# Transposes of 66 rows in place of 40 in the one-layer steps of a recurrent-memory transformer kernel

## The chip, the cores and the metric

The kernel runs on one core of one Trainium2 chip. The metric is the device time of one execution in microseconds (us); of several runs the median is taken. Besides these runs there is one profiled execution, which has its own time. In its trace every instruction has an engine, a line of the kernel, a start and a duration. The engines are PE (TensorE, matmuls), PEld (its weight loads), DVE (VectorE), ACT (ScalarE), POOL (GpSimd) and SP (SyncE, which here only issues DMAs).

## The reference: what is computed

Two layers of a transformer with a recurrent memory, each followed by a gated feed-forward network. The sequence of 2048 rows of width 512 is cut into 64 segments of 32 rows. Each segment is put behind 8 memory rows, so one segment has 40 rows (L = 40 in the code), and 32 heads of width 128 attend within these 40 rows. The first 8 rows of the attention's output are the memory of the next segment: that is the recurrence.

```python
for s in range(n_seg):                      # 64 segments
    xs = x[:, s * seg_len:(s + 1) * seg_len, :].copy()
    h = jnp.concatenate([mem, xs], axis=1)  # 8 + 32 rows
    q = jnp.einsum('btd,dhe->bhte', h, Wq)  # k and v likewise
    scores = jnp.einsum('bhqe,bhke->bhqk', q, k) * scale
    scores = jnp.where(mask[None, None], scores, -1000000000.0)
    p = _softmax(scores, axis=-1)
    o = jnp.einsum('bhqk,bhke->bhqe', p, v)
    o = jnp.einsum('bhte,hed->btd', o, Wo)
    mem = o[:, :M, :].copy()
    outs.append(o[:, M:, :])
...
x = x + A(_layernorm(x)); x = x + B(_layernorm(x))     # layer 0
x = x + A(_layernorm(x)); x = x + B(_layernorm(x))     # layer 1, same weights
```

B is `(sigmoid(x @ w_gate) * (x @ w_up)) @ w_down` with 1792 hidden columns. Data is bf16.

## The kernel before

**Steps.** The two layers run interleaved: step t (`emit_step`, L771) works on segment t of layer 0 and on segment t - 6 of layer 1 (LAG = 6), so there are 70 steps. Steps 6 to 63 are two-layer steps: the 40 rows of both layers stand side by side, 80 columns (`ncol` = 80, `both` true). Steps 0 to 5 have layer 0 alone and steps 64 to 69 layer 1 alone: these 12 are the one-layer steps, with `ncol` = 40. After every fourth step the feed-forward network of a block of 128 rows (`ffn`, L1050) is added for each layer, and projections of values (`v_pass`, `strips`, `v_half`) for later steps are spread among all of it.

**Inside a step.** The 32 heads are cut into groups. In one-layer steps there are two rows of 16 heads; a group takes three heads of each row (five groups of six heads), and the last group takes one of each (two heads). For each group:

- q and k for three heads at a time on PE (L868), copied to SBUF by ACT (L891, recorded at L1228), then the scores on PE (L904).
- Softmax: the mask is added on DVE (L918), the maximum taken (L923) and subtracted (L925), the exponential on ACT (L928), its sum (L930), its reciprocal (L932), and the weights written by DVE to the tile `pb` (L939, `pmul`). `pb` is 80 partitions by 3 by 128: a partition is a query row, and in one-layer steps each of the (up to) three blocks of 128 columns holds the 40 keys of two heads side by side, the rest zero.
- Transposes on PE (L950, `ptr`): for each block one transpose, whose stationary operand is the block and whose moving operand is a corner of the identity. `full` (L783) says how many partitions are read; it has the size `ncol`, so 40 in one-layer steps and 80 in two-layer steps. The result has 128 partitions and as many columns as rows were read, and block ul starts at column ul x 80 (LW = 80) of a PSUM bank.
- The copies out of PSUM to `ptsb` (L954, `spread`) on ACT or DVE, which read the first 40 columns of each 80; then weights times values on PE (L976), a copy on ACT (L985), and the output projection on PE (L995), which sums all heads of the step in one bank.

At the end of a step DVE copies the new memory rows into the input of the next step (L1013, in two-layer steps L1008), and ACT copies the others (L1020). The first q and k of the next step wait for it.

So a one-layer step has 5 x 3 + 1 = 16 transposes, and the 12 of them have 192. The 58 two-layer steps have 11 each, 638 in all, of 80 rows.

**Order.** All work is recorded as tasks with `pl.add(engine, duration, function, reads, writes)`. The order over all engines isn't searched for in the kernel: it is decoded from a packed list, `SEQUENCE` (L53, decoded in `plan`, L249), and with it for some copies the choice between ACT and DVE. The durations given to `pl.add` are used by `replay` (L268) only to reckon start times; from these come the pace at which POOL issues the large weight loads (a load waits for a PE task) and a few fill-in matmuls in reckoned gaps of PE (`warm`, L332). `mm_ns(n)` is the reckoned duration of a matmul with n columns. Each engine runs its own instructions in the order given and waits on semaphores for the others.

**Contents of `pb`.** Its three buffers are set to zero at the start (`clear`, L496). One-layer steps write partitions 0 to 39, two-layer steps 0 to 79.

## Time and profile before

| what | us |
|---|---|
| median of 3 runs | 1756.25 |
| lowest and highest of them | 1754.74, 1759.64 |
| profiled execution, its own time | 1757.29 |
| its span in the trace | 1755.3 |

Stretches of the same trace, by the view of windows:

| stretch, us from the start | what runs | length | PE busy |
|---|---|---|---|
| 60 to 172 | steps 0 to 5, with the end of the loading of weights at the front | 112.00 | 110.64 |
| 172 to 1624 | two-layer steps | 1452.00 | 1448.62 |
| 1624 to 1740 | steps 64 to 69 | 116.00 | 115.05 |

How to read it: the span is the time from the first to the last instruction in the trace; the time of an execution is a little more. Busy time of PE is the union of its matmuls, whose ends are modelled; matmuls overlap in the pipeline, so a single duration (some 180 to 200 ns for a small one) is far more than the distance from one start to the next, and it is this distance that PE pays for a matmul. In a form such as `40*128 40x40 bf16` the first number is the rows of the stationary operand (the contraction), the second its columns, and `40x40` is the moving operand, partitions by columns. A timeline row merges equal instructions that follow each other: its start, its duration to the end of the last, and how many. The granted clock is 1.00 (full) in all three stretches.

### The profile page before, as it was taken

The page shows a single profiled execution, that of the slowest core. Times are in us where ns is not written, and L with a number is a line of the kernel's source. Part 1 is how long each engine was busy: PE and PEld are TensorE (multiplying, and loading weights), DVE is VectorE, ACT ScalarE, POOL GpSimd, SP SyncE. Part 2 cuts the span into 40 slices and gives each one's busy share as a digit, 9 for nine tenths or more (in the row PEclk, how much of TensorE's full clock was granted, in tenths as well). Part 3 has the DMA queues.
Part 4 walks back from the last instruction along what each step waited for, and adds up shares of the span by engine and source line. Part 5 has one row for each costly group of instructions (what it writes and reads, how often), then busy time and mean ns, then how long its engine had stood idle before and what let it go on. Part 6 is the DMA issues. An engine that isn't in the chain of part 4 may idle for free.

```text
span 1755.3 us, 91842 instructions
## 1 busy us (share of the span) xinstructions
PE 1743.5 (99%) x39162; PEld 1496.5 (85%) x39162; DVE 1249.4 (71%) x4208; ACT 1129.5 (64%) x3119; POOL 856.8 (49%) x1367
## 2 busy tenths in 40 slices
PE   9999999999999999999999999999999999999999
PEld 4688889889898988989888888989888898989887
DVE  5667777677777776786677767776777777767676
ACT  3576777566666766666666656666665666666554
POOL 6524345635544554445455563554455463554443
PEclk9999999999999999999999999999999999999999
DMA  9935455635645555545455564545455464554644
GB/s 299 307 95 150 110 153 154 200 110 152 176 130 163 156 160 142 166 127 166 146 148 159 141 178 125 167 138 152 135 166 170 133 179 126 147 156 128 170 116 136
DMA packets 145583, 273.41 MB, mean 156 GB/s; under 512 B 39686, under 2 KB 86018, under 8 KB 145174
## 3 DMA queue, kind: packets, MB, share of 16 engines
q0 software_dynamic: 72944, 198.79, 39.6%
q1 hardware_dynamic: 72230, 68.75, 13.3%
q8 instruction: 307, 5.03, 1.2%
q14 instruction: 102, 0.84, 0.2%
HBM read 221.78 MB, written 27.07 MB: 142 GB/s over the span
## 4 chain that ended last, share of the span: by engine, by line
PE 96%; DMA 2%; DVE 1%; POOL 0%; SPq 0%; issue 0%; ACT 0%; POOLq 0%; ACTq 0%
PE bank L868 34%; PE bank L995 17%; PE bank L1097 11%; PE bank L762 8%; PE bank L635 7%; PE bank L1120 6%; PE bank L904 4%; PE bank L976 4%; PE bank L950 2%; PE bank L595 1%; PE bank L1214 1%; DMA wk_sb<-in_A_Wk_dram 1%; PE bank L1065 0%; DMA scr<-wu 0%; DMA wq_sb<-in_A_Wq_dram 0%
## 5 line engine op out<-in xcount | busy, mean ns | idle before, releaser
L868 PE MATMUL bank<-hT,wq_sb 128*128 128x80 bf16 (+3 forms) x8960 | 616.4, 198 | 2.4 <-DMA wq_sb<-in_A_Wq_dram 1.6
L868 PE MATMUL bank<-hT,wk_sb 128*128 128x80 bf16 (+3 forms) x8960 | 616.1, 198 | 1.0 <-DMA wk_sb<-in_A_Wk_dram 1.0
L1228 ACT CAST qku<-bank 128x480 bf16<-128x480 f32 (+4 forms) x770 | 384.6, 508 | 225.2 <-PE bank L868 196.2
L868 PEld LDWEIGHTS <-wq_sb 128*128 128x128 bf16 x8960 | 454.1, 99 | 33.7 <-issue 14.8
L868 PEld LDWEIGHTS <-wk_sb 128*128 128x128 bf16 x8960 | 446.8, 99 | 1.1 <-DMA wk_sb<-in_A_Wk_dram 1.1
L918 DVE TENSOR_TENSOR st<-bank,cst 40x240 f32<-40x240 f32 (+3 forms) x768 | 280.3, 368 | 116.5 <-PE bank L904 103.3
L995 PE MATMUL bank<-otsb,wo_sb 128*128 128x80 bf16 (+1 forms) x8960 | 360.4, 198 | 0.0
L995 PEld LDWEIGHTS <-wo_sb 128*128 128x128 bf16 x8960 | 335.9, 99 | 13.3 <-issue 0.2
L1228 ACT CAST otsb<-bank 128x480 bf16<-128x480 f32 (+3 forms) x420 | 200.4, 483 | 90.5 <-PE bank L976 60.3
L1090 POOL DMA_DIRECT2D wu<-in_B_w_up_dram x217 | 166.1, 766 | 172.2 <-PE bank L950 39.0
L1114 POOL DMA_DIRECT2D wd<-in_B_w_down_dram x217 | 156.5, 721 | 185.3 <-PE bank L1120 40.1
L1224 POOL DMA_DIRECT2D vsb<-sst x351 | 177.8, 511 | 130.5 <-ACT sst L1228 62.9
L1089 POOL DMA_DIRECT2D wg<-in_B_w_gate_dram x217 | 166.0, 765 | 140.6 <-PE bank L1097 58.8
L928 ACT ACTIVATE st<-st 80x240 f32<-80x240 f32 (+3 forms) x420 | 159.1, 381 | 56.5 <-DVE st L925 53.7
L1097 PE MATMUL bank<-xnT,wg 128*128 128x128 bf16 (+2 forms) x1784 | 171.6, 218 | 0.0
L1097 PE MATMUL bank<-xnT,wu 128*128 128x128 bf16 (+2 forms) x1784 | 171.0, 218 | 0.0
L930 DVE TENSOR_REDUCE small<-st 80x6 f32<-80x240 f32 (+3 forms) x420 | 151.3, 362 | 25.8 <-ACT st L928 22.3
L1220 ACT ACTIVATE ptsb<-bank,small 120x160 bf16<-120x160 bf16 (+3 forms) x430 | 156.7, 386 | 19.2 <-PE bank L950 12.5
L904 PE MATMUL bank<-qku 128*128 128x80 bf16 (+1 forms) x2240 | 162.8, 197 | 0.5 <-issue 0.4
L925 DVE TENSOR_TENSOR st<-st,small 80x240 f32<-80x240 f32 (+3 forms) x420 | 154.8, 370 | 5.7
L939 DVE TENSOR_TENSOR pb<-st,small 80x240 bf16<-80x240 f32 (+3 forms) x420 | 153.9, 369 | 5.7
L923 DVE TENSOR_REDUCE small<-st 80x6 f32<-80x240 f32 (+3 forms) x420 | 152.4, 363 | 6.2
(108 smaller groups left out, 2551.6 us busy)
## 6 DMA issues: line engine op xcount, KB each, us to landing
wg<-in_B_w_gate_dram POOLq DMA_DIRECT2D x220, 256.0 KB, 4.1
wu<-in_B_w_up_dram POOLq DMA_DIRECT2D x220, 256.0 KB, 4.2
wd<-in_B_w_down_dram POOLq DMA_DIRECT2D x220, 256.0 KB, 3.9
vsb<-scr SPq DMA_DIRECT2D x137, 66.0 KB
scr<-vst SPq DMA_DIRECT2D x90, 96.0 KB
vsb<-scr POOLq DMA_DIRECT2D x93, 66.0 KB, 3.5
vsb<-sst SPq DMA_DIRECT2D x179, 32.0 KB
vsb<-sst POOLq DMA_DIRECT2D x169, 32.0 KB, 2.8
```

The lines of the kernel that those rows point to most:

```text
L868: nc.tensor.matmul(o_ap, lhsT=W[:, c, h * P:(h + 1) * P], rhs=mv(c), start=(c == 0), stop=(c == DC - 1))
L904: nc.tensor.matmul(s_all(SB)[:, w0 + i, :], lhsT=fview(qku[:, i, 0, 0:1], [(1, P)]), rhs=qku[:, i, 1, 0:ncol], start=True, stop=True)
L918: pl.add("DVE", dve_ns(n, True), lambda gsz=gsz, hs=hs, st=st, SB=SB, pj_=pj_, npj_=npj_, mk=mk, idx=idx: nc.vector.tensor_tensor(out=st[p ...
L928: pl.add("ACT", act_ns(n), lambda hs=hs, st=st: nc.scalar.activation(out=st[pr, hs], in_=st[pr, hs], func=ACTF.Exp, scale=self.scale), r=s ...
L995: nc.tensor.matmul(WB[:, c * ncol:(c + 1) * ncol], lhsT=self.wo[:, h, c * P:(c + 1) * P], rhs=otsb[:, hl, 0:ncol], start=(h == 0 and c == ...
L1089: pl.add("POOL", 760, lambda wg=wg, fs=fs: nc.gpsimd.dma_start(out=wg[:], in_=self.wgv[:, :, fs]), r=[("wo", self.H - 1)], w=[gk] + bt, la ...
L1090: pl.add("POOL", 760, lambda wu=wu, fs=fs: nc.gpsimd.dma_start(out=wu[:], in_=self.wuv[:, :, fs]), r=[("wo", self.H - 1)], w=[uk] + bt, la ...
L1097: nc.tensor.matmul(gu[:, 2 * i + k, 0:n], lhsT=W[:, c, i * P:(i + 1) * P], rhs=xnT[:, c, rw], start=(c == 0), stop=(c == DC - 1))
L1114: pl.add("POOL", 760, lambda wd=wd, ip=ip: nc.gpsimd.dma_start(out=wd[:], in_=self.wdv[:, 2 * ip:2 * ip + 2, :]), w=[dk] + (["boot"] if se ...
L1220: nc.scalar.activation(out=dst, in_=src, func=ACTF.Copy, scale=by)
L1224: {"SP": nc.sync, "POOL": nc.gpsimd}[tk.on].dma_start(out=got[1], in_=got[2])
L1228: nc.scalar.copy(out=dst, in_=src)
```

## The change

The slice `full` becomes 66 in one-layer steps in place of 40; it stays 80 in two-layer steps. With it the transposes of one-layer steps read 66 partitions of `pb`, use a corner of the identity of 66 x 66, and write 66 columns of each block of 80 in PSUM. The duration given for the task is that of 66 columns.

```diff
-        full = slice(0, ncol)
+        full = slice(0, LW if both else 66)
...
                 for ul in range(nu):
-                    nc.tensor.transpose(out=pt[:, ul * LW:ul * LW + ncol], in_=pb[full, ul, :], identity=self.ident[full, full])
-
-            pl.add("PE", nu * mm_ns(ncol), ptr, r=[("pb", bi)], w=[PB])
+                    nc.tensor.transpose(out=pt[:, ul * LW:ul * LW + full.stop], in_=pb[full, ul, :], identity=self.ident[full, full])
+
+            pl.add("PE", nu * mm_ns(full.stop), ptr, r=[("pb", bi)], w=[PB])
```

The rows 40 to 65 that are now read hold zeros in steps 0 to 5, and in steps 64 to 69 what the last two-layer step that used the buffer left there. They meet the columns 40 to 65 of the identity, so they go to columns 40 to 65 of the result, which the copies to `ptsb` don't read. Every engine's list of instructions, and what each of them waits for, is the same in both programs; the 192 transposes (a load of weights and a matmul each) differ in size alone.

## The prediction

> **What bounds the kernel now.** I read the page first: busy time by engine, then the chain that ended last.

> ```profile
> PE 1743.5 (99%) x39162; PEld 1496.5 (85%) x39162; DVE 1249.4 (71%) x4208; ACT 1129.5 (64%) x3119; POOL 856.8 (49%) x1367
> ...
> PE 96%; DMA 2%; DVE 1%; POOL 0%; SPq 0%; issue 0%; ACT 0%; POOLq 0%; ACTq 0%
> ```

> TensorE (PE) issues nearly all the time, and 96% of the chain of waits is PE. But a busy PE can still be a slow one: a matmul counts as busy until its modelled end, so a hole of 0.1 us between two starts stays invisible here. The second reading is therefore where the changed transposes stand, by the view of line L950 in the two stretches of one-layer steps (60 to 180 us, and 1624 to 1740 us), and the busy time of those stretches.

> ```profile
> L950 PE MATMUL bank<-cst,pb x96: 176/176/190, 62.1 to 167.6; 40*128 40x40 bf16 x96
> ```

> ```profile
> L950 PE MATMUL bank<-cst,pb x96: 176/176/190, 1633.0 to 1736.8; 40*128 40x40 bf16 x96
> ```

> ```profile
> 60.00:172.00 112.00, 110.64 (x2908) 89.23 (x2909) 78.53 (x277) 77.30 (x279) 43.24 (x72) 1.00 0.55 162
> 172.00:1624.00 1452.00, 1448.62 (x32279) 1272.90 (x32268) 1047.50 (x3529) 956.47 (x2546) 716.96 (x1120) 1.00 0.53 150
> 1624.00:1740.00 116.00, 115.05 (x3273) 98.11 (x3272) 83.25 (x290) 69.28 (x230) 54.84 (x82) 1.00 0.53 149
> ```

> The columns are the stretch, its length, then busy us of PE, PEld, DVE, ACT, POOL, the granted clock, DMA share, GB/s. So 192 transposes of 40 rows exist, all in stretches where PE is busy for 110.64 of 112 us and 115.05 of 116 us at a clock of 1.00, while DVE and ACT are at 60 to 72%. What a PE instruction costs there is what the kernel pays.

> Third, the timeline of PE, starts in us, then duration. First 80-row transposes between other matmuls (a two-layer step), then 40-row ones (a one-layer step).

> ```profile
> 1612.64 0.31 PE L868 MATMUL bank<-hT,wq_sb 128*128 128x80 bf16 x4
> 1612.78 0.31 PE L868 MATMUL bank<-hT,wk_sb 128*128 128x80 bf16 x4
> 1612.93 0.24 PE L950 MATMUL bank<-cst,pb 80*128 80x80 bf16 x2
> 1613.01 0.31 PE L868 MATMUL bank<-hT,wq_sb 128*128 128x80 bf16 x4
> ```

> ```profile
> 1632.50 0.39 PE L1097 MATMUL bank<-xnT,wg 128*128 128x128 bf16 x4
> 1632.72 0.39 PE L1097 MATMUL bank<-xnT,wu 128*128 128x128 bf16 x4
> 1633.04 0.24 PE L950 MATMUL bank<-cst,pb 40*128 40x40 bf16 x3
> 1633.21 0.27 PE L868 MATMUL bank<-hT,wq_sb 128*128 128x40 bf16 x4
> ```

> Four 128-column matmuls take 0.22 us from start to start (1632.50 to 1632.72). Before the 40-row transposes the same four take 0.32 (1632.72 to 1633.04): 0.10 us of hole. Then three transposes hold PE for 0.17 us, though they are half as wide as the 80-row ones, two of which take 0.08. Around the 80-row ones nothing is lost: 0.14 to 0.15 us for the four in front, as for the four before. [...]

> **The change, part by part.** I call a run of L950 transposes with other matmuls on both sides a visit. The trace has 67 visits with 192 transposes of 40 rows: 10 of one transpose, 52 of three, 2 of four, 3 of six. All distances are from start to start.

> *Removed: the entry hole.* What stands before a visit normally moves on after 25 ns (L995, L904 and L868 at 40 or 54 columns), 35 (L976 at 80), 56 (L1097 at 128) or 216 (512 columns). Before a visit it takes 112, 111, 117, 130, 152 and 310. The excess is 87 to 96 ns, and 6.13 us over the 67.
> *Replaced: the transposes.* Inside a visit the 125 distances sum to 3.91 us (31 ns each); from a visit's last transpose to the next matmul it is 109 ns (122 in a visit of one), 7.58 us in all. Before: 6.13 + 3.91 + 7.58 = 17.62 us of PE.
> *Added: 26 columns and 26 rows.* No 66-row transpose is in the trace. Lower bound: a plain matmul with 66 columns (L868 128x66) moves on after 29 ns. Upper bound without a hole: an 80-row transpose with 80 columns takes 40. 66 columns lie a little nearer the first, so 33 inside a visit, and 29 for the last one, since the last of an 80-row visit goes at its plain matmul pace (35). After: 125 x 33 + 67 x 29 = 4.13 + 1.94 = 6.07 us; with 29 and 40 inside it is 5.57 and 6.94.
> *Does 66 behave as 80 or as 40?* Rows only: forms of 8, 32 and 40 rows show the hole of about 95 ns, 80, 96 and 120 rows do not. 66 lies nearer to 80, and in the same count of 32-row strips (three); I take 80's behaviour. The other end is 40's: holes kept, and 4 ns (29 - 25) x 192 = 0.8 us more.
> [...]

> PE's gain is 17.62 - 6.07 = **11.5 us** (10.7 to 12.0).

> *Moved, and new waits:* nothing. Each engine has the same instructions with the same waits; no queue and no DMA issue is touched. The unread columns 40 to 65 land in PSUM that nobody reads.

> *What of it is given back.* PE runs ahead by 0.17 us per visit, and what it waits for comes no sooner unless its own cause lies on PE too. For every PE wait on DVE or ACT I compared the release with the start in the trace. The transposes' own wait, for the product pb (L939), is over a median 687 ns early; 3 of 67 are under 100 ns (about 42 is the floor, and the hole is inside the figure). Those 3 lose up to 0.17 each: 0.5 us. Of the 430 DVE and ACT waits in the two stretches 83 are under 210 ns, mostly L904 behind ACT's copy of q and k, L976 and L995. They lose only where a visit lies between the wait and its cause; these causes are some 0.7 us back, and 67 visits in 228 us put 0.2 of a visit there: 83 x 0.2 x half of 0.17 = 1.4 us, less because a wait once paid loosens the next. I take 1.5 us together. If that cover were worse, ACT (copy before L904) and DVE (the five softmax operations) would be late next.
> The step boundary does not lose: where L868 of the next step starts at the 42 ns floor behind the copy of the memory rows (L1013), the chain from the last L995 to it holds no visit. DMA has room: the loads of wg, wu and wd land at least 0.67 us before PE wants them in these stretches, and after 172 us the gain of the first half only shifts the rest.

> Sum: 11.5 - 1.5 = **10.0 us**. The profiled execution, 1757.29 us (span 1755.3 and 2.0 around it), would become 1747.3. It lies 1.0 above the median of the runs; against the median 1756.25 - 10.0 = **1746.3 us**, 0.57% faster.

> **Rivals.**
> *The gain goes into waits.* PE arrives earlier and stands before DVE and ACT; half the gain or more is lost: 11.5 / 2, so about 1750.5. For it: 21 of those 430 waits are under 60 ns, and the recurrence binds at several step ends. Against: in these stretches the waits of PE that the profile lists sum to 2.1 us, and one at 60 us is a weight load.
> *The change doesn't do what it says.* The limit is above 66 rows, or the hole belongs to another trait of these transposes; 1756.25 + 0.8 = 1757. For: 66 is unseen. Against: 80, 96 and 120 rows are free, with partial strips too (80 and 120).
> *Slower: the weight load comes into the open.* Each transpose has its own load of pb rows, 92 to 103 ns (median 99), now hidden. If a load that reaches into the third strip cannot go ahead of the matmul in flight, each of 192 transposes pays 99 ns: 19.0 us for the 11.5 saved, 1756.25 + 7.5 = 1763.8. It decides from 60 ns a transpose (11.5 / 192). Against: 80-row loads of the same length reach the third strip and their transposes move on every 40 ns.
> [...]

> **How the numbers follow.** Forecast (7.5 us gained or more): 0.72. Gain into waits (2 to 7.5 us): 0.14. No effect: 0.08. Load in the open, or another loss: 0.06. 0.3% is 5.3 us, about what a measurement can tell from no change. Faster by more: 0.72 and some 0.08 of the second, 0.80. Within: the other 0.06, and 0.08 of no effect, 0.14. Slower: 0.06. The range must reach from the full 12.0 us with the runs' own scatter of 1.5 below the median (1742.8) to the second rival's worse part, 3.3 us gained: 1742.8 to 1753.

> **What would show it.** In the profile of the changed kernel: L950 as 66*128 x192; the four matmuls before it at their usual distance (0.22 for 128 columns); three transposes in 0.09 to 0.10 us instead of 0.17; the first stretch (60 to 172) and the last shorter by about 5 us each, the middle unchanged. Wrong if the 0.10 in front stays (limit above 66), if transposes stand 0.1 apart (load in the open), or if PE's waits on L1228 and L939 grow by more than 3 us (gain into waits).

## The result, and the profile after

The changed kernel was compared twice with the one before.

| comparison | after, median (lowest to highest) | before, median | ratio after/before (95% interval) |
|---|---|---|---|
| first, 6 runs each | 1748.01 (1746.70 to 1751.34) | 1758.28 | 0.9947 (0.9934 to 0.9960) |
| second, 12 and 17 runs | 1748.86 (1746.55 to 1757.22) | 1754.45 | 0.9969 (0.9957 to 0.9981) |

It is faster in both: by 10.3 us of the medians in the first, by 5.6 in the second. The two intervals overlap only from 0.9957 to 0.9960, some 7 us. In the second comparison four of the 12 runs after and one of the 17 before had a mean granted clock of 0.997 to 0.999; the medians of the others are 1748.07 and 1754.36. The profiled execution after took 1748.83 us with a span of 1747.1; before it was 1757.29 and 1755.3.

First the page of the profile after: busy time by engine, the queue that carries instructions (packets, MB, share), and the chain that ended last.

```profile
PE 1733.4 (99%) x39162; PEld 1491.8 (85%) x39162; DVE 1248.4 (71%) x4208; ACT 1128.5 (65%) x3119; POOL 859.0 (49%) x1367
...
q8 instruction: 307, 5.03, 1.2%
...
PE 94%; DMA 3%; DVE 1%; SPq 1%; issue 1%; POOL 0%; ACT 0%; POOLq 0%; ACTq 0%
```

PE still bounds the kernel, but its part of the chain fell from 96% to 94%; DMA has 3% and "issue" 1%, which stood at 2% and 0%. That is the first hint of where a part of the gain went. Queue q8, which carries instructions, comes back below.

The view of line L950 after, in the first and the last stretch:

```profile
L950 PE MATMUL bank<-cst,pb x96: 190/192/203, 62.7 to 164.8; 66*128 66x66 bf16 x96
```

```profile
L950 PE MATMUL bank<-cst,pb x97: 190/192/203, 1616.4 to 1728.1; 66*128 66x66 bf16 x96, 80*128 80x80 bf16 x1
```

Each transpose has become longer by itself (median 192 ns in place of 176), and the kernel shorter: a single duration is not what PE pays. The timeline of PE after, at the visit that the prediction showed in the kernel before:

```profile
1627.45 0.39 PE L1097 MATMUL bank<-xnT,wg 128*128 128x128 bf16 x4
1627.67 0.39 PE L1097 MATMUL bank<-xnT,wu 128*128 128x128 bf16 x4
1627.90 0.26 PE L950 MATMUL bank<-cst,pb 66*128 66x66 bf16 x3
1627.99 0.26 PE L868 MATMUL bank<-hT,wq_sb 128*128 128x40 bf16 x4
```

The four matmuls in front take 0.22 to 0.23 us (they took 0.32), and the three transposes 0.09 us (0.17). The holes on both sides are gone.

I measured all 67 visits in one way, which the experiments use too: the *visit sum* is the time from the start of the matmul in front of a visit to the start of the matmul behind it, added over the visits. It was 20.76 us before and is 9.88 after: 10.88 us less.

The windows after (length; busy us of PE, PEld, DVE, ACT, POOL; granted clock; DMA share; GB/s):

```profile
60.00:172.00 112.00, 109.87 (x2980) 89.23 (x2977) 79.83 (x281) 78.85 (x287) 46.41 (x79) 1.00 0.57 166
172.00:1624.00 1452.00, 1450.30 (x32373) 1274.83 (x32370) 1050.15 (x3537) 957.47 (x2550) 720.43 (x1123) 1.00 0.53 151
1624.00:1740.00 116.00, 113.19 (x3277) 97.91 (x3274) 83.43 (x295) 68.97 (x232) 54.73 (x81) 1.00 0.53 150
```

More matmuls fit into the first window (2980 for 2908), at the same clock, yet PE is busy for less of it: 2.1 us idle in place of 1.4, and 2.8 in place of 0.95 in the last. Fixed windows hold different work in the two kernels, so I also measured the time between the same matmuls, those which in the first trace of before start at 62, 172, 1624 and 1738 us:

| trace | 62 to 172 | 172 to 1624 | 1624 to 1738 |
|---|---|---|---|
| before, three traces | 110.04, 109.83, 109.65 | 1451.96, 1451.02, 1449.92 | 113.99, 113.07, 113.45 |
| after, four traces | 106.67, 108.73, 107.10, 105.26 | 1449.60, 1452.54, 1451.69, 1452.64 | 110.86, 109.79, 109.18, 109.41 |
| difference of the means | -2.9 | +0.65 | -3.7 |

The traces beyond the first pair are of runs named below. The middle only scatters: waits of 0.9 to 1.6 us come and go there in both kernels. The stretches with the changed transposes lose 6.6 us, of 10.9 us by which the visits became shorter. So some 4.3 us were given back inside the stretches.

What PE waited for after, from 60 to 1740 us (total us, times, longest):

```profile
PE bank L995 <- DMA wo_sb<-in_A_Wo_dram: 1.3, 3, 0.6
PE bank L904 <- issue: 0.9, 1, 0.9
PE bank L995 <- issue: 0.8, 2, 0.4
PE bank L868 <- DMA wk_sb<-in_A_Wk_dram: 0.6, 1, 0.6
PE bank L868 <- issue: 0.5, 2, 0.3
PE bank L762 <- issue: 0.3, 1, 0.3
PE bank L868 <- DVE hT L1008: 0.3, 1, 0.3
...
```

and before, the rows of the same view that end with "issue":

```profile
PE bank L904 <- issue: 0.4, 1, 0.4
PE bank L868 <- issue: 0.4, 2, 0.2
...
PE bank L762 <- issue: 0.3, 1, 0.3
```

"Issue" is time in which PE stands and waits for no semaphore: 1.1 us before, 2.5 in the rows shown after. The wait of L995 for wo, the weights of the output projection, does not show in this trace of before. No wait for pb (L939) shows in either kernel.

### The profile page after: what moved, and what is told of

Its sections match the earlier page's. It is cut to its first block, busy times and chain, and to the rows that moved or that the text cites. A ratio compares the mean times of both kernels' runs of the same rounds, so it can differ in the third digit from the quotient of the medians.

```text
span 1747.1 us, 91842 instructions
## 1 busy us (share of the span) xinstructions
PE 1733.4 (99%) x39162; PEld 1491.8 (85%) x39162; DVE 1248.4 (71%) x4208; ACT 1128.5 (65%) x3119; POOL 859.0 (49%) x1367
## 4 chain that ended last, share of the span: by engine, by line
PE 94%; DMA 3%; DVE 1%; SPq 1%; issue 1%; POOL 0%; ACT 0%; POOLq 0%; ACTq 0%
PE bank L868 34%; PE bank L995 17%; PE bank L1097 12%; PE bank L762 8%; PE bank L635 6%; PE bank L1120 6%; PE bank L904 4%; PE bank L976 4%; PE bank L950 2%; PE bank L595 1%; PE bank L1214 1%; DMA wk_sb<-in_A_Wk_dram 1%; DMA wo_sb<-in_A_Wo_dram 0%; PE bank L1065 0%; DMA scr<-wu 0%
## 5 line engine op out<-in xcount | busy, mean ns | idle before, releaser
L868 PE MATMUL bank<-hT,wq_sb 128*128 128x80 bf16 (+3 forms) x8960 | 616.4, 198 | 1.0 <-DVE hT L1008 0.3
L868 PE MATMUL bank<-hT,wk_sb 128*128 128x80 bf16 (+3 forms) x8960 | 616.3, 198 | 0.8 <-DMA wk_sb<-in_A_Wk_dram 0.6
L1228 ACT CAST qku<-bank 128x480 bf16<-128x480 f32 (+4 forms) x770 | 384.7, 508 | 223.7 <-PE bank L868 194.6
L868 PEld LDWEIGHTS <-wq_sb 128*128 128x128 bf16 x8960 | 454.2, 99 | 32.1 <-issue 15.1
L868 PEld LDWEIGHTS <-wk_sb 128*128 128x128 bf16 x8960 | 446.9, 99 | 1.1 <-DMA wk_sb<-in_A_Wk_dram 0.7
L995 PE MATMUL bank<-otsb,wo_sb 128*128 128x80 bf16 (+1 forms) x8960 | 360.2, 198 | 2.2 <-DMA wo_sb<-in_A_Wo_dram 1.3
L995 PEld LDWEIGHTS <-wo_sb 128*128 128x128 bf16 x8960 | 336.6, 99 | 15.5 <-DMA wo_sb<-in_A_Wo_dram 2.0
L1228 ACT CAST otsb<-bank 128x480 bf16<-128x480 f32 (+3 forms) x420 | 200.2, 483 | 83.4 <-PE bank L976 52.8
L1097 PE MATMUL bank<-xnT,wg 128*128 128x128 bf16 (+2 forms) x1784 | 171.5, 218 | 0.0
L1097 PE MATMUL bank<-xnT,wu 128*128 128x128 bf16 (+2 forms) x1784 | 171.1, 218 | 0.0
L1220 ACT ACTIVATE ptsb<-bank,small 120x160 bf16<-120x160 bf16 (+3 forms) x430 | 156.6, 386 | 17.2 <-PE bank L950 10.7
L904 PE MATMUL bank<-qku 128*128 128x80 bf16 (+1 forms) x2240 | 162.7, 197 | 1.0 <-issue 0.9
L939 DVE TENSOR_TENSOR pb<-st,small 80x240 bf16<-80x240 f32 (+3 forms) x420 | 154.1, 370 | 5.7
```

What stands on the lines that cost most here:

```text
L868: nc.tensor.matmul(o_ap, lhsT=W[:, c, h * P:(h + 1) * P], rhs=mv(c), start=(c == 0), stop=(c == DC - 1))
L904: nc.tensor.matmul(s_all(SB)[:, w0 + i, :], lhsT=fview(qku[:, i, 0, 0:1], [(1, P)]), rhs=qku[:, i, 1, 0:ncol], start=True, stop=True)
L995: nc.tensor.matmul(WB[:, c * ncol:(c + 1) * ncol], lhsT=self.wo[:, h, c * P:(c + 1) * P], rhs=otsb[:, hl, 0:ncol], start=(h == 0 and c == ...
L1097: nc.tensor.matmul(gu[:, 2 * i + k, 0:n], lhsT=W[:, c, i * P:(i + 1) * P], rhs=xnT[:, c, rw], start=(c == 0), stop=(c == DC - 1))
L1220: nc.scalar.activation(out=dst, in_=src, func=ACTF.Copy, scale=by)
L1228: nc.scalar.copy(out=dst, in_=src)
```

## The experiments

Two questions: what makes the hole, and what became of the 4.3 us. Edits are against the changed kernel. The times are medians, with the runs of the kernel before on the same chip beside them; e1 to e4 share one chip, e5 to e7 another.

| label | median | before on that chip | ratio (95%) | visit sum, us | median of a visit of three, ns |
|---|---|---|---|---|---|
| before | | | | 20.76 | 289 |
| after | | | | 9.88 | 115.5 |
| e1_rows64 | 1757.41 | 1755.74 | 1.0011 (1.0002 to 1.0020) | 21.89 | 308 |
| e2_rows80 | 1747.34 | 1755.74 | 0.9962 (0.9949 to 0.9974) | 10.9 | 137 |
| e3_40_66_40 | 1767.03 | 1755.74 | 1.0066 (1.0053 to 1.0079) | 33.1 | 497.5 |
| e4_66_40_66 | 1756.57 | 1755.74 | 1.0009 (1.0000 to 1.0018) | 21.12 | 312 |
| e5_first | 1751.30 | 1756.38 | 0.9977 (0.9966 to 0.9988) | | |
| e6_last | 1752.61 | 1756.38 | 0.9980 (0.9970 to 0.9989) | | |
| e7_shift32 | 1747.55 | 1756.38 | 0.9957 (0.9941 to 0.9972) | | |

**64 rows, and 80.**

```diff
-        full = slice(0, LW if both else 66)
+        full = slice(0, LW if both else 64)
```

> One-layer transposes of 64 rows and 64 columns: almost the size of the changed kernel (66), but on the other side of 64. Theory (PE empties for forms of at most 64 rows): the holes of 87 to 96 ns in front of the 67 visits and of about 80 behind them are there as before, the columns cost some 4 ns more each; time 0 to +1 us against the kernel before. Rival (the gain came with size, from 26 more rows and columns): the holes are gone, about -9 us.

```diff
-        full = slice(0, LW if both else 66)
+        full = slice(0, LW)
...
-            pl.add("PE", nu * mm_ns(full.stop), ptr, r=[("pb", bi)], w=[PB])
+            pl.add("PE", nu * mm_ns(LW if both else 66), ptr, r=[("pb", bi)], w=[PB])
```

> One-layer transposes of all 80 rows, the planner's duration left as with 66. Theory: no holes; distances of 36 to 40 ns in place of 29 to 31, so 192 x 8 = 1.5 us more PE work than with 66; time -8 to -10 us against the kernel before. Rival (66 is special, or wider transposes cost what the holes cost): not faster than -5 us.

With 64 rows the holes are back. The timeline of PE in that run:

```profile
1631.12 0.39 PE L1097 MATMUL bank<-xnT,wg 128*128 128x128 bf16 x4
1631.35 0.39 PE L1097 MATMUL bank<-xnT,wu 128*128 128x128 bf16 x4
1631.66 0.26 PE L950 MATMUL bank<-cst,pb 64*128 64x64 bf16 x3
1631.86 0.27 PE L868 MATMUL bank<-hT,wq_sb 128*128 128x40 bf16 x4
```

1631.35 to 1631.66 is 0.31 us for four matmuls that take 0.23 just above, and the transposes hold PE for 0.20. With 80 rows there is no hole, and the run is 10.1 us below that of 64 rows on the same chip, though every transpose is a quarter wider. So the price hangs on a limit above 64 and at or below 66 in the size of the transpose, not on the amount of work. Rows and columns were changed together in all these kernels; a kernel with 66 of the one and 40 of the other wasn't tried. The trace of the kernel before speaks against the 40 moving columns as the cause: plain matmuls of 128 rows by 40 columns stand next to wider ones without a hole (56 ns from a 128-column matmul to them, 25 ns from them to the next). What PE does during a hole was not shown: the traces have the distances between starts, and ends that are modelled.

The hole isn't a matter of transposes or of rows alone. The strips of the value projection (L762) have 128 rows, but a stationary operand of only 32 columns, and the trace of the kernel before has a hole on both sides of them:

```profile
1648.77 0.31 PE L904 MATMUL bank<-qku 128*128 128x40 bf16 x6
1649.01 1.91 PE L762 MATMUL bank<-wv_sb,hT 128*32 128x512 bf16 x32
1650.85 0.27 PE L868 MATMUL bank<-hT,wq_sb 128*128 128x40 bf16 x4
```

The six matmuls in front take 0.24 us where six of their kind take 0.15. Over the trace, by the medians, the distance into a strip is 109 ns after a matmul of 40 columns (25 otherwise) and 132 after one of 80 (36 otherwise), and out of it 312 ns (206 from one four of a strip to the next). All 73 strips keep these holes in the changed kernel.

**Both forms within one visit.**

```diff
                 for ul in range(nu):
-                    nc.tensor.transpose(out=pt[:, ul * LW:ul * LW + full.stop], in_=pb[full, ul, :], identity=self.ident[full, full])
+                    f = full if both else slice(0, (L, 66)[ul % 2])
+                    nc.tensor.transpose(out=pt[:, ul * LW:ul * LW + f.stop], in_=pb[f, ul, :], identity=self.ident[f, f])
```

> Within a visit the transposes alternate: 40 rows, 66 rows, 40 rows. Theory (the cost is a change of form, once in and once out): a visit of three enters and leaves the 40-row form twice, 60 more pairs of holes than before at 0.17 us each; +9 to +11 us against the kernel before, though only 132 of 192 transposes have 40 rows. Rival (each 40-row transpose costs by itself, 11.5 us / 192 = 60 ns): 60 of them are cheaper, -3.6 us.

The same with `(66, L)[ul % 2]`, so that a visit of three begins and ends with 66 rows:

> The same the other way round: 66, 40, 66 rows; the ten visits of one have 66. Theory (change of form): 60 pairs of holes in place of 67, so -1 to -2 us against the kernel before. Rival (cost of each 40-row transpose): 60 in place of 192 of them, -8 us.

The timeline of PE with 40, 66, 40 rows (the row merges the two forms; line numbers are one higher):

```profile
1635.59 0.39 PE L1098 MATMUL bank<-xnT,wu 128*128 128x128 bf16 x4
1635.90 0.45 PE L951 MATMUL bank<-cst,pb 40*128 40x40 bf16 x3
1636.28 0.27 PE L868 MATMUL bank<-hT,wq_sb 128*128 128x40 bf16 x4
```

Three transposes now hold PE for 0.38 us, and the visit has four holes in place of two. From start to start the visits of three have, by the medians, 117 ns in front, 122 and 136 between its transposes, 122 behind. With 66, 40, 66 rows it has 25 in front and 39 behind, and 124 and 122 inside. So the hole belongs to the change from one form to the other, at each change, also between two transposes: it is not a price of entering or leaving the transposes, nor one of a narrow transpose as such, since those in an unbroken run of 40 rows are 31 ns apart. Its time tells the same: 12.3 us more in the visits of e3 than before, +11.3 us of the medians. For e4 I expected a little less than before; it came out by 0.8 us above, with a visit sum that is 0.36 above and not below.

**Only the first stretch, only the last.**

```diff
-        full = slice(0, LW if both else 66)
+        full = slice(0, LW if both else 66 if t < LAG else L)
```

> 66 rows in steps 0 to 5 alone, 40 in steps 64 to 69. Theory: half of the holes go (33 of 67 visits, about -5.5 us), of which up to 2 us may be given back to weights (wo) that have not landed when PE comes to them at 65 to 79 us; -3.5 to -5.5 us against the kernel before. If the changed kernel's loss of about 1.5 us there was only that run's scatter: -5.5.

The other with `t > LAG`:

> 66 rows in steps 64 to 69 alone. Theory A (PE's instructions arrive too late: in the changed kernel's trace PE stands 0.2 to 1.1 us, with no wait for a semaphore, at every place in the last stretch where its instruction number is 195 modulo 256, and more of it than before): -5.5 us of holes, +2.5 us of such stands; -3 to -3.5 us against the kernel before. Theory B (waits on ACT and DVE as forecast, or scatter): -4.5 to -5.5 us.

The first half alone gains 5.1 us of the medians (2.1 to 6.0 by the interval), the last alone 3.8 (1.9 to 5.3). Together 8.9, so the two halves add up to the whole as well as such intervals can tell; they don't by themselves tell how much was given back. The 3.8 of e6 lie between the two theories for it; and in the changed kernel's first trace, PE stood by over 0.1 us at 8 of the 26 places that theory A names in the last stretch, not at every one. The trace of e6, whose profiled execution was its slowest run (1754.83), shows something else: its last stretch took 113.40 us, as before the change. The timeline of PE there:

```profile
1684.12 0.25 PE L868 MATMUL bank<-hT,wk_sb 128*128 128x40 bf16 x4
1686.12 0.32 PE L904 MATMUL bank<-qku 128*128 128x40 bf16 x6 [1.75 <-issue]
1686.37 2.95 PE L762 MATMUL bank<-wv_sb,hT 128*32 128x512 bf16 x32
```

and the windows around it:

```profile
1683.70:1687.10 3.40, 1.66 (x50) 1.19 (x49) 1.56 (x5) 1.00 (x3) 0.16 (x1) 1.00 0.55 155
1687.10:1690.50 3.40, 3.40 (x61) 1.79 (x54) 2.38 (x7) 0.99 (x2) 0.25 (x1) 0.50 0.02 5
1690.50:1694.00 3.50, 3.50 (x122) 3.50 (x119) 3.18 (x13) 2.34 (x8) 2.04 (x4) 1.00 0.51 111
```

PE stands for 1.75 us without a semaphore to wait for, and afterwards the granted clock is 0.50 for 3.4 us; a strip of 32 matmuls takes 2.95 us where the others of its kind take 1.91. The stand has eaten 1.9 us and the half clock 1.3 more. The same fall of the clock is in one other trace of the fourteen, e9 (the changed kernel again, below), after three waits for wo within 2.5 us (0.86, 0.49 and 0.18 us):

```profile
75.40:78.80 3.40, 1.87 (x45) 1.39 (x45) 0.19 (x1) 0.98 (x3) 2.41 (x6) 1.00 0.92 304
78.80:82.20 3.40, 3.40 (x82) 3.40 (x79) 0.00 (x0) 1.08 (x4) 3.40 (x7) 0.50 0.74 221
```

There the q and k matmuls from 78.79 us on, 1.93 us in the other three traces after, took 3.42: 1.5 us more. A stand is not always followed by it: after the 1.32 us in e5 the clock stayed at 1.00.

```diff
                     B, n = fill[tk.idx]
+                    for _ in range(16 if tk.idx == min(fill) else 0):
+                        nc.tensor.matmul(B[:, 0:32], lhsT=self.hot[:], rhs=self.hot[:, 0:32], start=True, stop=True)
```

> The changed kernel with 16 small fill-in matmuls (32 PE instructions) more in PE's first microseconds, where it waits for weights anyway. Theory A (the stands belong to places in the instruction stream): every stand without a semaphore moves 32 instructions earlier in the program, so to other lines, and stays at 195 modulo 256 of the new numbers; time that of the changed kernel within 1 us, about -10 us against the kernel before. Theory B (they belong to the work at those lines): they stay at the same matmuls.

Where stands came in e7, they kept their number in the list and so moved 32 instructions in the work. One example is number 74,435, in a strip of the value projection. In the kernel before it stands after the 20th matmul of the strip:

```profile
1669.94 1.26 PE L762 MATMUL bank<-wv_sb,hT 128*32 128x512 bf16 x20
1671.51 0.83 PE L762 MATMUL bank<-wv_sb,hT 128*32 128x512 bf16 x12 [0.31 <-issue]
```

and with the 32 instructions ahead, after the 4th:

```profile
1663.78 0.40 PE L762 MATMUL bank<-wv_sb,hT 128*32 128x512 bf16 x4
1664.76 1.69 PE L762 MATMUL bank<-wv_sb,hT 128*32 128x512 bf16 x28 [0.58 <-issue]
```

So such a stand is not tied to the matmul that PE is at. But whether one comes at a given number varies: number 75,459, where PE stood in all nine other full traces (by 0.6 to 1.9 us), has none in e7. In the ten traces with a full record of PE, I took all crossings of such a place after 62 us. At 73 of them PE stood by over 0.1 us; 62 of these end 1.17 to 1.60 us after a packet of q8 has landed. At the other 2957 crossings the last packet has been there for a median of 3.8 us, and only 9 of them were passed less than 1.17 us after a landing. By these counts PE waits for its own instructions at these stands. The time of e7 is that of the changed kernel: the stands moved and their sum (4.6 us) did not fall.

**The two kernels again, for their traces and for the time.** No edit: before twice, after twice, then after with times.

> The kernel before, unchanged, for a second trace. If stands of PE at 194 or 195 modulo 256 (instructions that come late) grow with PE's pace in the one-layer steps, they sum to 1.5 to 2.7 us here, as in the four traces with holes in the last stretch; no wait for wo over 0.4 us. If they are scatter that has nothing to do with the change: anything from 0.6 to 5 us, and a wait for wo as likely as not.

> The changed kernel, unchanged, for a second trace. Growing with pace: stands of 3 to 5 us, and PE waits 0.9 to 2 us for wo between 65 and 80 us. Scatter: as in the kernel before.

> As for the second trace of the kernel before: 1.5 to 2.7 us of stands, no wait for wo over 0.4 us, if they grow with pace; else anything from 0.6 to 5.

> As for the second trace of the changed kernel: 3 to 5 us of stands, 0.9 to 2 us for wo, if they grow with pace; else as in the kernel before.

> The changed kernel, unchanged, timed again. If the give-back is what the six traces of the two kernels show (2 to 2.5 us of late instructions and about 1 us of waits for wo, out of 10.9 us of holes), -7 to -8.5 us against the kernel before. If the first measurement (-10.3 between the medians) is the size of it, and the give-back only some 0.5 us, -9.5 to -11 us.

The sums of PE's stands at such places in the two one-layer stretches (starts beyond the usual distance, so somewhat more than the idle time in the view of waits), and its waits for wo, in us:

| | stands | waits for wo |
|---|---|---|
| before, three traces | 2.05, 0.92, 0.88 | 0, 0, 0.3 |
| after, four traces | 4.44, 3.28, 3.92, 2.95 | 1.3, 1.5, 0.8, 0.2 |
| other kernels without holes: e2, e7 | 2.68, 4.6 | 0.9, 0.6 |
| other kernels with holes: e1, e3, e4 | 2.53, 0.55, 2.28 | 0, 0, 0 |
| holes in one stretch only: e5 (last), e6 (first) | 2.8, 5.3 | 1.0, 0.2 |

The kernel before came out lower than I had expected in both traces (e8, e10), the stands of the changed one as expected (e9, e11); of its waits for wo the 0.8 fell just short. The profiled executions of these four took 1756.92 and 1754.71 us (before), 1751.31 and 1747.80 (after). The gain of e12, 5.6 us, is smaller than both forecasts for it; its interval (3.3 to 7.5) reaches into the first and excludes the second. The mean stand is 1.28 before and 3.65 after, 2.4 us more. All six traces without holes lie above all six with them, though only just (2.68 against 2.53), so the direction is borne out and the size is not sharp. Taken by stretch the two kinds overlap: e5 has 2.7 of its 2.8 us in the last stretch, where its holes are, and e2 only 1.4 there without any. Two of the stands after, by the timeline of PE:

```profile
1719.84 0.18 PE L868 MATMUL bank<-hT,wq_sb 128*128 128x40 bf16 x1
1720.30 0.24 PE L868 MATMUL bank<-hT,wq_sb 128*128 128x40 bf16 x3 [0.28 <-issue]
...
1728.80 0.36 PE L995 MATMUL bank<-otsb,wo_sb 128*128 128x40 bf16 x8
1729.61 0.76 PE L995 MATMUL bank<-otsb,wo_sb 128*128 128x40 bf16 x24 [0.45 <-issue]
```

They stand amid a run of equal matmuls, all of whose operands are there: after the first of four, after the eighth of 32. And the wait for wo:

```profile
77.49 0.47 PE L995 MATMUL bank<-otsb,wo_sb 128*128 128x40 bf16 x12 [0.49 <-DMA wo_sb<-in_A_Wo_dram]
```

The first uses of wo, in step 0, come while the weights are still being loaded; PE arrives earlier and waits for them. That is 0.95 - 0.1 = 0.85 us on the mean. The half kernels agree: 1.0 in e5, which has no holes in the first stretch, and 0.2 in e6, which has them.

No kernel among these is clearly better than the changed one: e2 and e7 lie within its intervals.

## Why the prediction was right, and where its size was off

The forecast was 1746.3 us, 10.0 less than before. The medians are 1748.01 and 1748.86, and the gain by the overlap of the two intervals is about 7. That the first comparison gave 10.3 is partly luck: in the traces the two stretches became 6.6 us shorter, and three more runs had raised the median of the kernel before by 2.0 us over the one that the prediction started from.

- *PE bounds the kernel, and what a transpose costs is the distance between starts.* Right. The duration of one rose from 176 to 192 ns while the visits fell from 20.76 to 9.88 us.
- *The hole belongs to the 40-row form, and 66 behaves as 80.* Right. With no row between 40 and 80 in the trace of before, the side of 66 was my estimate, and the strips of 32 rows by which I counted show in no trace; now the side is shown: 64 rows have the hole (visit sum 21.89 us), 66 and 80 have not (9.88 and 10.9). Sharper than I had it: the price is that of each change between forms (e3, e4).
- *Gain of PE, 11.5 us (10.7 to 12.0).* It was 10.88. The prediction left the usual distance in front of the visits out of its sum; that is 20.76 - 17.62 = 3.14 us, so 9.88 - 3.14 = 6.74 stand against the 6.07 that I had put. The clean distances are slightly better than taken (29 to 31.5 ns inside, for 33; 29 behind, as taken); a few visits hold a wait of 70 to 250 ns, and these make the difference.
- *Nothing new is waited for, and 1.5 us are given back.* This is the term that was mis-sized: the stretches gave back about 4.3 us. Of these 2.4 are PE standing for its own instructions, which was no part of the sum at all, though four small "issue" waits of PE were to be read before the change. 0.85 are waits for wo: I had checked that wg, wu and wd land early, and overlooked wo. Of the 1.05 that are left, 1.5 / 4 = 0.4 are the half clock in one of the four traces after (e9), which no term foresaw either. Some 0.7 remain for the small waits on DVE and ACT, which I had put at 1.5; they were not followed one by one.
- *Rival, the gain goes into waits (1750.5).* Its direction was partly right and its mechanism not: it named DVE and ACT, and neither holds the larger part. Its sign, growth of the waits on L1228 and L939 by over 3 us, didn't come.
- *Rival, no effect (1757).* Fell: it is what 64 rows do (e1, 1.7 us above before by the medians).
- *Rival, the weight load comes into the open (1763.8).* Fell: transposes of 66 rows follow each other every 29 to 31.5 ns, and their loads take 96 (the median of the last stretch after), so these stay hidden.
- *Signs.* L950 as 66*128 x192, 0.22 in front, 0.09 for three: as listed. The stretches shorter by about 5 us each: only in part, they lost 2.9 and 3.7. The middle unchanged: within its scatter.

What stays open: the size of the gain lies between the 5.6 and the 10.3 us of two comparisons. That faster visits raise the stands is carried by twelve traces whose two kinds nearly touch, and why a packet of instructions is late at one place and not at the next was not looked into; no kernel took the stands away.

## What to carry to other kernels

Look at starts, not at durations, where a small matmul stands among large ones: a form of 40 or 64 rows between full ones cost this kernel some 90 ns on each side, which no busy time shows, and padding it to 66 rows of zeros or stale data, with columns nobody reads, was worth more than the added work. Keep neighbours on one side of the step that lay between 64 and 66 rows here: forms of 40 and 66 rows that alternate paid at every change (122 to 136 ns from start to start, for 29 to 31.5 in an unbroken run), while forms of 66, 80 and 128 rows stood beside each other for nothing (25 ns from a 40-column matmul of 128 rows into a transpose of 66, 29 out of it; 35 or 36 between 80-column matmuls of 128 rows and transposes of 80). When PE gets faster, list *all* that it consumes as what may be late next: every weight tensor near its first use, and its own instructions.

## What the runs showed of the hardware that I had not expected

- PE can stand for its instructions in the middle of a run of matmuls, by 0.1 to 1.9 us, in the one-layer stretches always at the same place modulo 256 in its list (194 or 195); 62 of 73 such stands ended 1.17 to 1.60 us after a 16 KB packet had landed. At the 25 ns from one 40-column matmul to the next, 256 instructions (128 matmuls and their weight loads) last by my estimate only 128 x 25 ns = 3.2 us; at 56 ns (128 columns) 7.2 us.
- After a stand of 1.9 us in the middle of full work (e6), and after three waits of 1.5 us in sum (e9), the granted clock was 0.50 for 3.4 us; what made it fall was not shown. The strip of 32 matmuls that met it in e6 took 2.95 us in place of 1.91.
- A change of form costs the same between two transposes (122 to 136 ns from start to start) as between a transpose and a full matmul of 40 columns (112 to 122). The strips with 32 stationary columns pay a like price on both sides: 84 or 96 ns more on the way in (109 for 25, 132 for 36), 106 on the way out (312 for 206).
